# Squares' buffers moved to the front of SBUF in a fused block-attention and squared-ReLU kernel

## The chip, the cores and the metric

One NeuronCore of a Trainium2 chip. The metric is device time in microseconds (us) of one launch. The kernel before took 622.73 us (median of three runs, 622.30 to 624.28).

## The reference

Attention over q, k, v of shape (4 batches, 8 heads, 768 positions, 64), then a two-layer network on the 3072 tokens of width 512. Every query sees the keys less than 16 positions away and, besides, one summary of each 32-key block (the maximum of the keys, the mean of the values).

```python
k_sum = k.reshape(B, H, nb, block, D).max(axis=3)
v_sum = v.reshape(B, H, nb, block, D).mean(axis=3)
scores_all = np.concatenate([scores_l_m, scores_s], axis=-1)   # masked local, summary + log(32)
a = softmax(scores_all)
x = a @ np.concatenate([v, v_sum], axis=2)                     # (3072, 512) after the heads are joined
h = np.maximum(x @ w_in, 0.0)                                  # w_in (512, 2048)
out = (h * h) @ w_out                                          # w_out (2048, 512)
```

## The kernel before, in words

The 3072 tokens are 24 tiles of 128; two tiles make a chunk of 256 tokens, so there are 12 chunks. Every float32 matrix of the network is kept as a high and a low part in float32r, and a product is three matmuls: high by high, low weights by high, high weights by low.

**First layer** (`ffn1`, L384 to L393): for one of the 16 blocks f of 128 hidden units, 12 matmuls of 256 columns. The weights loaded into TensorE are 128 columns of `w_sb[f]`, the moving operand is a 256-column piece of `xh` or `xl` (L390). A slot does two f, so 24 matmuls. **Second layer** (`ffn2`, L427 to L437): for one f, two halves of 128 tokens by three matmuls of 512 columns. Here the weights loaded are 128 columns of the squares `gh` or `gl`, and the moving operand is the second half of a row of `w_sb[f]` (L434). A slot has 12 of them. Between the layers ScalarE takes the ReLU (L398) and the high square (L404), VectorE the square (L409) and its low part (L412).

For the first two chunks the order of every instruction is written out by hand in the string START (L42 to L69): weights are unpacked there and the attention of the first six tiles is done. After that `slot` (L468 on) runs 8 slots per chunk: 24 first-layer matmuls, then the 12 second-layer matmuls of the slot before, and beside them the attention of the two tiles that come next, which VectorE, ScalarE and GpSimd do; its matmuls (L277, L360) stand at the end of the 8 slots. `tc.manual_schedule` keeps this order on each engine.

**Where things lie in SBUF.** A pool lays its tiles one behind the other, in steps of 32 bytes per partition, in the order in which they are first asked for. Three pools follow each other: `const` (L86 to L110), `big` (18 slots of 8192 bytes, in which the unpacked weights `w_sb[f]` end up), and `work` (the small `nmx` and `total`, then `xh`, `xl`, `ob`). Tiles named gap are read and written by nothing and only take room. In the built program before, bytes from the start of a partition: `gh` 48128, `gl` 52224, the slots of `big` from 56896 on, `nmx` from 204352, `total` from 204544, `xh` 204768 and 208864, `xl` 212960 and 217056, `ob` from 221152 to 229344. Inside a weight slot the low part begins 4096 bytes, the second layer's half 2048 bytes, the next 128 columns 512 bytes further on; pieces of `xh` and `xl` and the four squares in `gh` and `gl` are 1024 bytes apart, the two token halves of a square 512.

`mask_max` (L297 to L308) takes a tile `nmx` from a ring of six for every half of a token tile's heads; `exponentials` (L310) reads it, `inverse` (L317 on) gives it back.

Of the kernel before, what the change touches and what calls it, by code (L numbers as in the profile page):

```python
# [11 lines left out]
F32 = mybir.dt.float32  # L12
F32R = mybir.dt.float32r
# [11 lines left out]
P = 128  # L25
# [3 lines left out]
CT = TPC * P  # L29
# [43 lines left out]
def attn_ffn_kernel(ctx: ExitStack, tc: tile.TileContext, q, k, kt, v, vt, x0, w, consts, out):  # L73
# [3 lines left out]
    const = ctx.enter_context(tc.tile_pool(name="const", bufs=1))  # L77
    big = ctx.enter_context(tc.tile_pool(name="big", bufs=1))
    work = ctx.enter_context(tc.tile_pool(name="work", bufs=2))
# [3 lines left out]


    w_sb = {}
    consts_sb = const.tile([P, 3 * NK + P + 8 * 32], F32, name="consts_sb")  # L86
    mask_sb = consts_sb[:, 0 : 3 * NK].rearrange("q (m c) -> q m c", m=3)
    id_sb, mean_sb = consts_sb[:, 3 * NK : 3 * NK + P], consts_sb[:, 3 * NK + P :]
# [9 lines left out]
    ksums = [const.tile([P, NPAIR, NB], F32, name=f"ksum{i}") for i in range(2)]  # L98
    vsum = const.tile([P, NPAIR, 32], F32, name="vsum")
    r_sb = [const.tile([P, DM], F32, name=f"r{i}") for i in range(2)]  # L100
    const.tile([P, 56], F32, name="gap0")
    gh_sb = const.tile([P, 4, CT], F32R, name="gh")
    gl_sb = const.tile([P, 4, CT], F32R, name="gl")

    sm_sb = const.tile([P, 8, 4, 2], F32, name="sm")
    zero = const.tile([P, 1], F32R, name="zero")
    zero32 = const.tile([P, 1], F32, name="zero32")
    junk = const.tile([P, 1], F32, name="junk")

    const.tile([P, 56], F32, name="gap")  # L110


    bank = [ps_s.tile([P, DM], F32, name=n, tag=f"{n}{i}") for i, n in enumerate(["s_ps"] * 4 + ["ph"] * 2)]
# [8 lines left out]
    def e_sb(g):  # L122
        return e_bufs[g % 2 if g < FROM_PAIRS else 0]
# [142 lines left out]
    s_ps, nmx, sm = {}, {}, {}  # L266
# [30 lines left out]
    def mask_max(g, h):  # L297

        t = g % NT
        m = mask_sb[:, 0 if t == 0 else 2 if t == NT - 1 else 1, :]  # L300
        half, i = divmod(h, 4)
        if (g, half) not in nmx:
            nmx[g, half] = work.tile([P, 4], F32, name="nmx", tag="nmx", bufs=6)
            sm[g, half] = sm_sb[:, (2 * g + half) % 8]
        nc.vector.tensor_tensor_reduce(  # L305
            out=e_sb(g)[:, h, 0:NK], in0=s_ps[g, half][h % 2][:, h // 2, 0:NK], in1=m, scale=-scale, scalar=3.0e38,
            op0=ALU.add, op1=ALU.min, accum_out=nmx[g, half][:, i : i + 1],
        )  # L308
# [8 lines left out]
    def softmax(g, h0, h1):  # L317

        for h in range(h0, h1):
            mask_max(g, h)  # L320
            exponentials(g, h)
# [250 lines left out]
    def begin(op, i, j, eng, at):  # L572
# [19 lines left out]
        elif op == "S":  # L592
            (scores_kt if i < FROM_KT else scores)(i, 2 * j, 2 * j + 2, at)
        elif op == "TT":
            mask_max(i, j)
        elif op == "E":
            exponentials(i, j)
# [150 lines left out]
```

## Time and profile before

| what | value |
|---|---|
| median of three runs | 622.73 us |
| the profiled execution's own time | 622.01 us |
| its span, first to last instruction | 619.9 us |
| TensorE matmuls busy | 607.6 us, 98% of the span |
| VectorE / ScalarE / GpSimd busy | 389.8 / 267.4 / 106.2 us |
| granted TensorE clock, mean | 0.999 of full speed |

A matmul's record includes its way through the array, and records overlap: TensorE's pace is the distance from one matmul's start to the next one's. The chain of work that ended last gives it without overlap, as stretches between starts.

### The profile page before, as it was taken

The numbers are of one execution on the slowest core, as the hardware profiler recorded it, in microseconds if no ns is written. First come the engines' busy times: TensorE is split into PE (matmuls) and PEld (weight loads), VectorE is DVE, ScalarE is ACT, GpSimd is POOL, SyncE is SP. The second block draws the span as 40 slices with busy tenths as digits, with TensorE's granted clock in tenths as the row PEclk, the third lists the DMA queues.
The fourth block names the chain that finished last, engine by engine and source line by source line (L and its number), as shares of the span: only waits on it lengthen the run. The fifth ranks groups of instructions, "written<-read, shape, count | busy, mean of one in ns | idle before, by whom it ended". The sixth has DMA issues, their size and how long they took to land.

```text
span 619.9 us, 12969 instructions
## 1 busy us (share of the span) xinstructions
PE 607.6 (98%) x5253; PEld 546.5 (88%) x5253; DVE 389.8 (63%) x1063; ACT 267.4 (43%) x688; POOL 106.2 (17%) x98
## 2 busy tenths in 40 slices
PE   7799999999999999999999999999999999999997
PEld 6589899789899999999999989999989989998996
DVE  6898998777637837747545845864663763663121
ACT  4898983234243432433425325425424424422212
POOL 4655466202000101102101101002101010110000
PEclk9999999999999999999999999999999999999999
DMA  8998141560007006006005204202201400300000
GB/s 329 410 413 336 52 136 52 153 193 30 1 9 264 2 2 220 2 2 221 1 2 188 86 1 126 97 1 76 95 2 38 133 1 1 87 1 1 35 1 34
DMA packets 21643, 59.41 MB, mean 96 GB/s; under 512 B 2256, under 2 KB 2256, under 8 KB 20048
## 3 DMA queue, kind: packets, MB, share of 16 engines
q1 hardware_dynamic: 21584, 58.59, 26.9%
q8 instruction: 41, 0.67, 0.4%
q14 instruction: 18, 0.15, 0.1%
HBM read 52.29 MB, written 6.29 MB: 94 GB/s over the span
## 4 chain that ended last, share of the span: by engine, by line
PE 93%; DVE 2%; ACT 2%; DMA 2%; SPq 1%; issue 0%; POOL 0%; DVEq 0%; POOLq 0%
PE o_ps L434 42%; PE ph L390 39%; PE s_ps L390 5%; PE ph L360 3%; PE s_ps L277 3%; DMA consts_sb<-in_consts 1%; ACT e_sb L313 1%; DVE w_sb L262 1%; PE s_ps L360 1%; DMA kv<-in_kt 0%; PE o_ps L159 0%; DVE v_sb L126 0%; SPq L180 0%; DVE ksum L188 0%; PE s_ps L339 0%
## 5 line engine op out<-in xcount | busy, mean ns | idle before, releaser
L390 PE MATMUL ph<-xh,w_sb 128*128 128x256 f32 x1360 | 246.8, 282 | 0.5 <-DVE xl L377 0.5
L434 PE MATMUL o_ps<-w_sb,gh 128*128 128x512 f32 x768 | 239.0, 392 | 0.0
L390 PEld LDWEIGHTS ph<-xh,w_sb 128*128 128x128 f32 x1360 | 213.4, 188 | 8.6 <-issue 1.4
L390 PE MATMUL ph<-xl,w_sb 128*128 128x256 f32 x680 | 190.5, 280 | 0.0
L434 PEld LDWEIGHTS o_ps<-w_sb,gh 128*128 128x128 f32 x768 | 137.6, 188 | 25.2 <-issue 0.2
L409 DVE TENSOR_TENSOR ph<-ph,r 128x512 f32<-128x512 f32 x83 | 58.1, 699 | 151.7 <-ACT r L398 150.9
L434 PE MATMUL o_ps<-w_sb,gl 128*128 128x512 f32 x384 | 151.2, 394 | 0.0
L398 ACT ACTIVATE r<-ph 128x512 f32<-128x512 f32 x83 | 49.2, 594 | 199.7 <-PE ph L390 199.7
L390 PEld LDWEIGHTS ph<-xl,w_sb 128*128 128x128 f32 x680 | 128.7, 189 | 0.0
L346 DVE STREAM_TRANSPOSE pT<-e_sb 32x256 f32<-32x256 f32 x240 | 104.6, 436 | 4.1 <-POOL e_sb L333 0.7
L313 ACT ACTIVATE e_sb<-e_sb,nmx 128x120 f32<-128x120 f32 x192 | 73.8, 386 | 68.8 <-DVE nmx L305 68.8
L333 POOL TENSOR_TENSOR e_sb<-e_sb,total 128x480 f32<-128x480 f32 x46 | 46.3, 1014 | 325.8 <-DVE total L327 181.3
L434 PEld LDWEIGHTS o_ps<-w_sb,gl 128*128 128x128 f32 x384 | 72.2, 188 | 15.3
L404 ACT ACTIVATE gh<-r 128x512 fp32r<-128x512 f32 x94 | 59.4, 632 | 11.9 <-DVE r L400 6.8
L412 DVE TENSOR_TENSOR gl<-ph,gh 128x512 fp32r<-128x512 f32 x83 | 57.4, 692 | 8.7 <-DVE ph L409 0.5
L253 POOL TENSOR_TENSOR w_raw<-w_raw 128x1024 int32<-128x1024 int32 (+1 forms) x20 | 34.1, 1712 | 35.6 <-DVE w_raw L248 18.1
L305 DVE CUSTOM_DVE_ANT_0 e_sb<-s_ps,consts_sb 128x120 f32<-128x120 f32 x172 | 38.8, 277 | 0.6 <-DMA consts_sb<-in_consts 0.2
L313 ACT ACTIVATION_READ_ACCUMULATOR e_sb<-e_sb,nmx 128x1 f32 x192 | 36.2, 188 | 0.0
L390 PE MATMUL s_ps<-xh,w_sb 128*128 128x256 f32 x176 | 32.5, 283 | 0.4 <-DVE w_sb L262 0.4
L390 PEld LDWEIGHTS s_ps<-xh,w_sb 128*128 128x128 f32 x176 | 27.5, 188 | 1.6 <-DVE w_sb L262 0.8
L377 DVE TENSOR_TENSOR xl<-ph,xh 128x512 fp32r<-128x512 f32 x19 | 13.1, 691 | 23.3 <-ACT xh L374 23.3
L390 PE MATMUL s_ps<-xl,w_sb 128*128 128x256 f32 x88 | 24.7, 281 | 0.0
(89 smaller groups left out, 419.0 us busy)
## 6 DMA issues: line engine op xcount, KB each, us to landing
w_raw<-in_w SPq DMA_DIRECT2D x12, 1024.0 KB, 11.7
k_sb<-in_k SPq DMA_DIRECT2D x20, 384.0 KB, 6.3
v_sb<-in_v SPq DMA_DIRECT2D x20, 384.0 KB, 4.7
kv<-in_kt SPq DMA_DIRECT2D x16, 384.0 KB, 5.7
q_sb<-in_q SPq DMA_DIRECT2D x24, 256.0 KB, 6.2
out<-ob SPq DMA_DIRECT2D x24, 256.0 KB, 2.1
kv<-in_vt SPq DMA_DIRECT2D x12, 384.0 KB, 6.3
w_raw<-in_w SPq DMA_DIRECT2D x8, 512.0 KB, 8.8
```

The costliest lines, as they stand in the source:

```text
L253: nc.gpsimd.tensor_tensor(out=lo, in0=hi, in1=lo, op=ALU.add)
L305: nc.vector.tensor_tensor_reduce(out=e_sb(g)[:, h, 0:NK], in0=s_ps[g, half][h % 2][:, h // 2, 0:NK], in1=m, scale=-scale, scalar=3.0e38, o ...
L313: nc.scalar.activation(e, e, AF.Exp, bias=nmx[g, half][:, i : i + 1], scale=-1.0, accum_out=sm[g, half][:, i, 0:1])
L333: eng.tensor_mul(out=e, in0=e, in1=sm.pop((g, half)).unsqueeze(2).to_broadcast([P, 4, NK]))
L346: nc.vector.transpose(out=pT[g % 2][j * 32 : j * 32 + 32, :, i * 32 : i * 32 + 32], in_=e_sb(g)[i * 32 : i * 32 + 32, :, j * 32 : j * 32 + ...
L360: nc.tensor.matmul(xp[o : o + 64, h // 2, s * 64 : s * 64 + 64], lhsT=values(g)[:, s, h * 64 : h * 64 + 64], rhs=pT[g % 2][:, h, s * 64 : ...
L390: nc.tensor.matmul(ph, lhsT=w_sb[f][:, w, cc * P : (cc + 1) * P], rhs=x[c][:, cc, :], start=(n == 0), stop=(n == 3 * NC4 - 1))
L398: nc.scalar.activation(r, ph, AF.Relu)
L404: nc.scalar.activation(gh, r, AF.Square)
L409: nc.vector.tensor_mul(out=ph, in0=ph, in1=r)
L412: nc.vector.tensor_sub(out=gl, in0=ph, in1=gh.bitcast(F32))
L434: nc.tensor.matmul(o_ps[c][tt], lhsT=g_[:, ts_], rhs=w_sb[f][:, w, DM:], start=(first and n == 0), stop=(last and n == 2),)
```

## The change

The two tiles of the squares move from behind the ReLU results to the front of the `const` pool, with a gap of 128 bytes ahead of them in place of one of 224; the gap at the end of that pool shrinks from 224 to 64 bytes; the ring of `nmx` gets a seventh tile. No instruction is added, taken away or moved.

```diff
     w_sb = {}
+    const.tile([P, 32], F32, name="gap0")
+    gh_sb = const.tile([P, 4, CT], F32R, name="gh")
+    gl_sb = const.tile([P, 4, CT], F32R, name="gl")
     consts_sb = const.tile([P, 3 * NK + P + 8 * 32], F32, name="consts_sb")
...
     r_sb = [const.tile([P, DM], F32, name=f"r{i}") for i in range(2)]
-    const.tile([P, 56], F32, name="gap0")
-    gh_sb = const.tile([P, 4, CT], F32R, name="gh")
-    gl_sb = const.tile([P, 4, CT], F32R, name="gl")
-
     sm_sb = const.tile([P, 8, 4, 2], F32, name="sm")
...
-    const.tile([P, 56], F32, name="gap")
+    const.tile([P, 16], F32, name="gap")
...
-            nmx[g, half] = work.tile([P, 4], F32, name="nmx", tag="nmx", bufs=6)
+            nmx[g, half] = work.tile([P, 4], F32, name="nmx", tag="nmx", bufs=7)
```

## Rows read from the trace of the kernel before

**Rows 1.** The profiled page: the span, TensorE's and the other engines' busy time, and the chain of work that ended last.
```profile
span 619.9 us, 12969 instructions
PE 607.6 (98%) x5253; PEld 546.5 (88%) x5253; DVE 389.8 (63%) x1063; ACT 267.4 (43%) x688; POOL 106.2 (17%) x98
...
PE 93%; DVE 2%; ACT 2%; DMA 2%; SPq 1%; issue 0%; POOL 0%; DVEq 0%; POOLq 0%
```

**Rows 2.** What TensorE waited for over the whole span, the longest two: us in total, times, longest.
```profile
PE s_ps L293 <- DMA q_sb<-in_q: 1.9, 2, 1.2
PE o_ps L566 <- issue: 1.3, 1, 1.3
```

**Rows 3.** Groups of instructions over the span, one form each: the matmuls of the two layers (busy us, mean ns | idle before).
```profile
L390 PE MATMUL ph<-xh,w_sb 128*128 128x256 f32 x1360 | 246.8, 282 | 0.5 <-DVE xl L377 0.5
L434 PE MATMUL o_ps<-w_sb,gh 128*128 128x512 f32 x768 | 239.0, 392 | 0.0
L390 PE MATMUL ph<-xl,w_sb 128*128 128x256 f32 x680 | 190.5, 280 | 0.0
L434 PE MATMUL o_ps<-w_sb,gl 128*128 128x512 f32 x384 | 151.2, 394 | 0.0
L390 PE MATMUL s_ps<-xh,w_sb 128*128 128x256 f32 x176 | 32.5, 283 | 0.4 <-DVE w_sb L262 0.4
L390 PE MATMUL s_ps<-xl,w_sb 128*128 128x256 f32 x88 | 24.7, 281 | 0.0
```

**Rows 4.** The chain in order of time in the middle and near the end of the steady stretch: start us, us, what.
```profile
331.35 2.85 PE ph L390 x24
334.19 2.76 PE o_ps L434 x12
...
602.25 2.85 PE ph L390 x24
605.10 2.76 PE o_ps L434 x12
```

**Rows 5.** Two stretches of the steady state, the second without attention: us, then busy us (x count) of PE, PEld, DVE, ACT, POOL, then the granted clock, DMA share and GB/s.
```profile
173.50:562.80 389.30, 388.82 (x3266) 352.67 (x3265) 235.93 (x687) 151.21 (x430) 34.81 (x38) 1.00 0.20 66
562.80:611.00 48.20, 48.20 (x314) 44.10 (x315) 11.83 (x17) 11.42 (x20) 0.00 (x0) 1.00 0.03 12
```

**Rows 6.** The timeline of TensorE at the start: 16 matmuls whose two operands are one broadcast zero, at the full clock (start us, us from the first start to the last end), and the last of them alone.
```profile
4.80 3.66 PE L566 MATMUL o_ps<-zero 128*128 128x512 f32 x16
...
8.08 0.38 PE L566 MATMUL o_ps<-zero 128*128 128x512 f32 x1
```

**Rows 7.** The timeline of TensorE over an ordinary first-layer slot: its third matmul, and the start of the second layer.
```profile
179.34 0.28 PE L390 MATMUL ph<-xl,w_sb 128*128 128x256 f32 x1
...
181.94 0.63 PE L434 MATMUL o_ps<-w_sb,gh 128*128 128x512 f32 x2
182.41 0.39 PE L434 MATMUL o_ps<-w_sb,gl 128*128 128x512 f32 x1
```

**Rows 8.** The same over the slot just before it, whose first matmuls came after those of the attention.
```profile
173.22 0.28 PE L277 MATMUL s_ps<-k_sb,q_sb 64*64 64x120 f32 x4
...
173.77 0.28 PE L390 MATMUL ph<-xl,w_sb 128*128 128x256 f32 x1
...
176.35 0.62 PE L434 MATMUL o_ps<-w_sb,gh 128*128 128x512 f32 x2
176.81 0.39 PE L434 MATMUL o_ps<-w_sb,gl 128*128 128x512 f32 x1
```

**Rows 9.** The same over a first-layer block of START, after a wait of TensorE for the unpacked weights.
```profile
68.32 0.39 PE L390 MATMUL s_ps<-xh,w_sb 128*128 128x256 f32 x1 [0.17 <-DVE w_sb L262]
68.54 0.28 PE L390 MATMUL s_ps<-xl,w_sb 128*128 128x256 f32 x1
...
69.74 0.63 PE L434 MATMUL o_ps<-w_sb,gh 128*128 128x512 f32 x2
```

**Rows 10.** The timeline of TensorE over one slot's second layer: the two token halves of one f, then of the next.
```profile
345.24 0.63 PE L434 MATMUL o_ps<-w_sb,gh 128*128 128x512 f32 x2
...
345.95 0.62 PE L434 MATMUL o_ps<-w_sb,gh 128*128 128x512 f32 x2
...
346.63 0.62 PE L434 MATMUL o_ps<-w_sb,gh 128*128 128x512 f32 x2
...
347.32 0.62 PE L434 MATMUL o_ps<-w_sb,gh 128*128 128x512 f32 x2
...
348.01 0.40 PE L390 MATMUL ph<-xh,w_sb 128*128 128x256 f32 x2
```

**Rows 11.** The records of the first layer's matmuls of `xh`: count, shortest/median/longest ns, first and last start, forms.
```profile
L390 PE MATMUL ph<-xh,w_sb x1360: 277/281/393, 35.2 to 610.3; 128*128 128x256 f32 x195
```

**Rows 12.** The line of `mask_max`: its instructions, and what its engine sat idle for before them (us, times).
```profile
L305 DVE CUSTOM_DVE_ANT_0 e_sb<-s_ps,consts_sb x172: 253/278/284, 10.7 to 543.7; 128x120 f32<-128x120 f32 x172
...
  DMA consts_sb<-in_consts: 0.2, 1
```

**Rows 13.** Groups of the page: the ReLU and the square between the layers (busy us, mean ns | idle of the engine before it and what ended most of that).
```profile
L409 DVE TENSOR_TENSOR ph<-ph,r 128x512 f32<-128x512 f32 x83 | 58.1, 699 | 151.7 <-ACT r L398 150.9
L398 ACT ACTIVATE r<-ph 128x512 f32<-128x512 f32 x83 | 49.2, 594 | 199.7 <-PE ph L390 199.7
```

## The prediction, written before the changed kernel was run

> **What bounds the kernel now.** I read the page first: matmuls are busy for 98% of the span, and the chain that ended last runs through TensorE for 93% of it [rows 1]. Next the waits of TensorE: the longest two sum to 3.2 us out of 619.9 [rows 2], so no other engine, queue or buffer can give back more than a few us. What is left is TensorE's own pace, so the third view is the chain in order of time, which counts from start to start. A slot of the steady state is 24 first-layer matmuls in 2.85 us and 12 second-layer matmuls in 2.76 us [rows 4]: 118.8 ns for 256 columns, 230 ns for 512. At the granted full clock of 2.4 GHz [rows 5] the columns alone are 106.7 and 213.3 ns. So each matmul loses 12 and 17 ns beyond its columns.
>
> Is that loss a fixed cost? Three views say no. (a) The matmuls of zeros at the start, with both operands broadcast from one element, start every (8.08 - 4.80) / 15 = 0.219 us [rows 6]: 5.4 ns beyond the columns, not 17. (b) The pace of the first layer depends on how it was entered. From the third matmul of an ordinary slot to the third of the second layer it is 182.41 - 179.34 = 3.07 us [rows 7]; in the slot entered from the attention's matmuls the same 24 distances take 176.81 - 173.77 = 3.04 [rows 8]; and in a block of START entered after a wait, ten distances take 69.74 - 68.54 = 1.20 us, 120 ns each [rows 9]. Same shapes, same clock, same offsets between operands, three paces. (c) It is not the other engines: the pace is 2.85 and 2.76 in the last 48 us too [rows 4], where VectorE is busy 11.8 and GpSimd 0 us [rows 5]. My reading: while one matmul streams its moving operand, the weights of the next are loaded, and the two reads disturb each other by their addresses and by their offset in time. The rows show the second of these; the first is inferred, and it is what the change acts on.
>
> **The change part by part.** It moves no instruction; the sum consists of what addresses do.
>
> *The new places.* From the tile sizes in steps of 32 bytes: the front now holds 128 + 8192 bytes more, so everything from `consts_sb` to `r` moves up by 8320. The weight slots begin at 56896 - 8192 - 224 - 224 + 8192 + 128 + 64 = 56640. `work` follows 256 bytes lower, less 32 for the seventh `nmx`: `xh` moves from 204768 to 204544. `gh` moves from 48128 to 1280. Distances:
> - `xh` minus weights: 147872 before, 147904 after. That is 32 bytes more, by any period: 416 becomes 448 modulo 512. All 2304 first-layer matmuls see it (1360 + 680 + 176 + 88 in [rows 3]).
> - weights minus `gh`: 8768 before, 55360 after. Modulo 512 both are 64; modulo 1024, 576 becomes 64. All 1152 second-layer matmuls (768 + 384 in [rows 3]).
> - `xl` minus `gh`, which meet once a slot where the second layer's first weights are loaded: 480 becomes 0 modulo 512.
>
> *Second layer: nothing.* The two token halves of a square lie 512 bytes apart, so before the change already half the matmuls stand at 576 and half at 64 modulo 1024. After the slot's first half, the halves take 346.63 - 345.95 = 0.68, 0.69 and 0.69 us [rows 10]: no difference between them. The move swaps which half has which distance. Bounds, were it otherwise: records in that group average 392 for `gh` and 394 ns for `gl` [rows 3]; 2 ns on 1152 is 2.3 us either way.
>
> *First layer: 32 bytes.* No row shows this distance, so I bound it. Below: the shortest record is 277 ns against a median of 281 [rows 11]; if every matmul lost only that, 4 x 2304 = 9.2 us gained. The pace of the zeros, 106.7 + 5.4 = 112.1 ns, would give (118.8 - 112.1) x 2304 = 15.4 us, but its operands stay on one element, so I keep it as a far end. Above: the pace of 120 ns [rows 9] everywhere costs 1.2 x 2304 = 2.8 us; no row of a whole block is slower. The value I take is the faster regime that this kernel already has when the two reads start at another offset [rows 8], since a shift of 32 bytes is a shift of offset between the reads too: 0.03 us for 24 distances. Of 2304 / 24 = 96 slots' worth, 12 (the first of each chunk) have it already, so 84 x 0.03 = 2.5 us. The readings are to 0.01 us, so it is 1.7 to 3.4.
>
> *The joint.* The first half of the second layer takes 345.95 - 345.24 = 0.71 us where later ones take 0.69 [rows 10]; with the new `xl` to `gh` distance the 0.02 us may go: 84 x 0.02 = 1.7 us at most, part of it counted in the 0.03 above. I take 0.7; the other bound is as much lost.
>
> *The seventh `nmx` and the gaps: nothing.* `mask_max` never sat idle for a buffer, only 0.2 us for a DMA [rows 12]. Tiles that nothing reads cost nothing.
>
> *Other engines' operands: nothing.* The squares are written by ScalarE and VectorE at other addresses. If that slowed them, the cover is large: ScalarE's ReLU stood idle 199.7 us waiting for TensorE, and VectorE's square 150.9 us for the ReLU [rows 13]. No DMA is added or reordered.
>
> The sum: 2.5 + 0.7 = 3.2 us less. The profiled execution took 622.01 us, 0.72 less than the median; 622.73 - 3.2 = 619.5 us.
>
> **The rivals.**
> *No change.* The two reads do not meet by address at all, and the three paces come from timing alone: whatever TensorE's reads wait for would then be the same at every distance, and the time 622.7 us. For it: slots at all 16 weights and both buffers of `xh` have the same 2.85 us [rows 4], and the second layer's halves agree across 512 bytes [rows 10]; it takes 32-byte effects to survive where 512-byte and larger ones do nothing. Against it: the zeros' pace [rows 6]. The Trainium skill ("SBUF — State Buffer", "Who interferes with whom") states a rule to the same end: TensorE has two independent read ports, one for the moving operand and one for loading weights, and never waits on anyone. By that rule the sum is 0 us. The trace neither confirms nor excludes it: three paces at one set of distances say that the two streams are coupled, not that addresses couple them.
>
> *Slower.* The new distance puts the ordinary slots into the slow regime. Place: L390's matmuls in all slots not entered from the attention. Price: 120 against 118.8 ns [rows 9, 4], 84 x 24 x 1.2 = 2.4 us, and the joint 0.7 lost instead of gained: 625.8 us. It decides as soon as the ordinary slot's 24 matmuls take over 2.86 us. For it: the slow regime lasts over a block once entered [rows 9], and a distance picked for other contents of SBUF has no reason to suit this one. Against: only one block of START is seen in it, while the fast one comes back at the head of every chunk [rows 8].
>
> *The change moves the second layer instead.* If the period of the effect is over 512 bytes after all, 230 ns changes by 2 to 4 ns: 2.3 to 4.6 us either way; shared out to the cases by sign.
>
> **How the numbers follow.** A measurement of this kernel tells 0.3% from no change, 1.9 us. Faster by more: 0.47, because the fast regime is in the trace and the room below (9.2, at the far end 15.4 us) is wider than above (2.8 to 4.6). Within 1.9 us: 0.25, the first rival and small shifts. Slower by more: 0.28. The predicted time is that of the likeliest case, 619.5 us, whose own range is 612 to 620.8. The whole range reaches up over no change to the slow regime with the second layer's bound on top, 622.7 + 2.4 + 0.7 + 2.3 = 628.1, and down to 622.7 - 9.2 - 1.7 = 611.8: 612 to 628 us.
>
> **What would show it.** In the chain of the changed kernel the ordinary slot's first-layer stretch of 24 should read 2.82 us, and the second layer's 12 stay at 2.75 to 2.76. If 24 read 2.85 and 2.76 again, the first rival holds; 2.88 is the second. If 12 matmuls of the second layer move from 2.76 by more than 0.02, my reading of the 512-byte period was wrong. If TensorE's pace is unchanged and the time is not, it must show as a wait of TensorE that is not in [rows 2], and all of the above is wrong.

## The result

613.17 us (median of four runs, 612.82 to 613.26) against 622.61 (now four runs of the kernel before): ratio 0.984, 95% interval 0.982 to 0.986. The profiled execution took 612.82 us with a span of 610.7, 9.2 us less than before [rows 1]. So the change made the kernel faster by about 1.5%, inside the range of the forecast and on its side, but by 9.4 us where 3.2 were forecast. The granted clock is 0.999 in the profiles of both kernels.

### The profile page after: what moved, and what is told of

The parts are those of the page before. It is cut to its first block, busy times and chain, and to the rows that moved or that the text cites. A ratio compares the mean times of both kernels' runs of the same rounds, so it can differ in the third digit from the quotient of the medians.

```text
span 610.7 us, 12969 instructions
## 1 busy us (share of the span) xinstructions
PE 598.4 (98%) x5253; PEld 537.8 (88%) x5253; DVE 389.8 (64%) x1063; ACT 267.5 (44%) x688; POOL 106.3 (17%) x98
## 4 chain that ended last, share of the span: by engine, by line
PE 91%; DVE 3%; ACT 3%; DMA 2%; issue 1%; SPq 0%; POOL 0%; DVEq 0%; ACTq 0%; POOLq 0%
PE o_ps L433 42%; PE ph L389 38%; PE s_ps L389 3%; PE ph L359 3%; PE s_ps L276 3%; DVE w_sb L261 1%; ACT e_sb L312 1%; DMA q_sb<-in_q 1%; PE s_ps L359 1%; ACT w_raw L236 1%; DMA kv<-in_kt 1%; PE o_ps L158 0%; DVE v_sb L125 0%; SPq L179 0%; DVE ksum L187 0%
## 5 line engine op out<-in xcount | busy, mean ns | idle before, releaser
L389 PE MATMUL ph<-xh,w_sb 128*128 128x256 f32 x1360 | 239.3, 278 | 0.6 <-DVE xl L376 0.5
L433 PE MATMUL o_ps<-w_sb,gh 128*128 128x512 f32 x768 | 238.0, 391 | 0.0
L389 PEld LDWEIGHTS ph<-xh,w_sb 128*128 128x128 f32 x1360 | 211.0, 188 | 8.9 <-issue 1.4
L389 PE MATMUL ph<-xl,w_sb 128*128 128x256 f32 x680 | 188.3, 277 | 0.0
L433 PEld LDWEIGHTS o_ps<-w_sb,gh 128*128 128x128 f32 x768 | 137.1, 188 | 25.1 <-issue 0.2
L433 PE MATMUL o_ps<-w_sb,gl 128*128 128x512 f32 x384 | 151.3, 394 | 0.0
L389 PEld LDWEIGHTS ph<-xl,w_sb 128*128 128x128 f32 x680 | 127.8, 188 | 0.0
L433 PEld LDWEIGHTS o_ps<-w_sb,gl 128*128 128x128 f32 x384 | 72.2, 188 | 14.6 <-DVE gl L411 0.3
L389 PE MATMUL s_ps<-xh,w_sb 128*128 128x256 f32 x176 | 31.5, 279 | 0.7 <-DVE w_sb L261 0.7
L389 PEld LDWEIGHTS s_ps<-xh,w_sb 128*128 128x128 f32 x176 | 27.1, 188 | 1.9 <-DVE w_sb L261 1.1
L389 PE MATMUL s_ps<-xl,w_sb 128*128 128x256 f32 x88 | 24.4, 277 | 0.0
```

Of the source, the lines that this page charges most:

```text
L389: nc.tensor.matmul(ph, lhsT=w_sb[f][:, w, cc * P : (cc + 1) * P], rhs=x[c][:, cc, :], start=(n == 0), stop=(n == 3 * NC4 - 1))
L433: nc.tensor.matmul(o_ps[c][tt], lhsT=g_[:, ts_], rhs=w_sb[f][:, w, DM:], start=(first and n == 0), stop=(last and n == 2),)
```

## The profile after the change

The page of the changed kernel: span, busy time, then the first layer's groups (L389 and L433 are the lines that were L390 and L434), to be set beside [rows 1, 3].

```profile
span 610.7 us, 12969 instructions
PE 598.4 (98%) x5253; PEld 537.8 (88%) x5253; DVE 389.8 (64%) x1063; ACT 267.5 (44%) x688; POOL 106.3 (17%) x98
...
L389 PE MATMUL ph<-xh,w_sb 128*128 128x256 f32 x1360 | 239.3, 278 | 0.6 <-DVE xl L376 0.5
L433 PE MATMUL o_ps<-w_sb,gh 128*128 128x512 f32 x768 | 238.0, 391 | 0.0
L389 PE MATMUL ph<-xl,w_sb 128*128 128x256 f32 x680 | 188.3, 277 | 0.0
L433 PE MATMUL o_ps<-w_sb,gl 128*128 128x512 f32 x384 | 151.3, 394 | 0.0
```

The counts are the same and the other engines work as long as before; the first layer's mean record went from 282 and 280 to 278 and 277 ns. The chain in order of time, as in [rows 4]:

```profile
129.62 2.94 PE ph L389 x24
132.56 2.75 PE o_ps L433 x12
...
338.13 2.75 PE ph L389 x24
340.88 2.75 PE o_ps L433 x12
343.62 2.75 PE ph L389 x24
...
593.29 2.75 PE ph L389 x24
596.04 2.75 PE o_ps L433 x12
```

A slot is 5.49 to 5.50 us where it was 5.61: 0.10 from the first layer, 0.01 from the second. In the kernel before, the first steady slot began here:

```profile
130.28 3.02 PE ph L390 x24
```

From there to the end it took 619.9 - 130.28 = 489.6 us, now 610.7 - 129.62 = 481.1: 8.5 of the 9.2 us lie in the 80 steady slots (80 x 0.11 = 8.8), 0.7 in START. Inside one slot, the timeline of TensorE, as in [rows 7]:

```profile
177.84 0.28 PE L389 MATMUL ph<-xl,w_sb 128*128 128x256 f32 x1
...
178.54 0.28 PE L389 MATMUL ph<-xl,w_sb 128*128 128x256 f32 x1
...
180.24 0.28 PE L389 MATMUL ph<-xl,w_sb 128*128 128x256 f32 x1
180.35 0.62 PE L433 MATMUL o_ps<-w_sb,gh 128*128 128x512 f32 x2
180.81 0.39 PE L433 MATMUL o_ps<-w_sb,gl 128*128 128x512 f32 x1
181.04 0.62 PE L433 MATMUL o_ps<-w_sb,gh 128*128 128x512 f32 x2
```

From 178.54 to 180.24 are 15 distances: 113.3 ns each, 1.2 above the 112.1 worked out from the zeros [rows 6]. The six distances before it take 0.70 us, 117 ns each: a slot begins at about the old pace and within its first matmuls locks into the new one. The second layer's first half takes 181.04 - 180.35 = 0.69 us where it took 0.71 [rows 10].

## The experiments

Distances are modulo 512 bytes: X is `xh` minus weights, Y is weights minus `gh`. The kernel before has X 416, Y 64; the changed one X 448, Y 64. The theory: X and Y set the paces, because the moving operand and the next weights are read at once. Its rivals are named where they are tested.

**Which part of the change does it?** Three kernels. The seventh ring tile without moving the squares (from the kernel before):

```diff
-    const.tile([P, 56], F32, name="gap0")
+    const.tile([P, 40], F32, name="gap0")
...
-            nmx[g, half] = work.tile([P, 4], F32, name="nmx", tag="nmx", bufs=6)
+            nmx[g, half] = work.tile([P, 4], F32, name="nmx", tag="nmx", bufs=7)
```

> The squares stay behind the ReLU results, as before; the nmx ring gets its seventh tile and the gap ahead of the squares is 64 bytes smaller, so that xh minus weights is 147904 (448 modulo 512, as in the changed kernel) and weights minus gh 8768 (as before). Distance theory (moving operand to weights decides): the whole gain is here, 24 first-layer matmuls in 2.75 us, 12 second-layer ones in 2.75, about 613 us. Alignment theory (xh begins at a multiple of 64 bytes): the same, since xh is at 204736. Squares theory (their place at the front, 64 instead of 576 modulo 1024, decides): 2.85 and 2.76, 622 us.

The same with 48 in place of 40 floats, so that the same distances begin 32 bytes off a multiple of 64:

> As the kernel before, with a seventh nmx tile and the gap ahead of the squares 32 bytes smaller: weights and squares lie 32 bytes lower, xh and xl stay at 204768 and 212960. Distances as in the run with the seventh tile and 64 bytes less (448 and 64 modulo 512), but every one of these tiles now begins 32 bytes off a multiple of 64. Distance theory: 2.75 us for 24, about 613 us. Alignment theory: 2.85 us, 622 us.

And the changed kernel with the ring back at six:

```diff
-            nmx[g, half] = work.tile([P, 4], F32, name="nmx", tag="nmx", bufs=7)
+            nmx[g, half] = work.tile([P, 4], F32, name="nmx", tag="nmx", bufs=6)
```

> The changed kernel with six nmx tiles again, so that xh and xl lie 32 bytes lower: xh minus weights 416 modulo 512 as before, squares at the front. Distance theory: the gain is gone, 2.85 us for 24 and about 622 us. Alignment theory: gone as well, xh is at 204512. Squares theory: the gain stays, 2.75 us and 613 us.

Measured: 613.04 (ratio 0.984, 0.981 to 0.986), 613.10 (0.984, 0.982 to 0.986) and 622.24 us (0.999, 0.998 to 1.001). The chains, in this order:

```profile
333.14 2.75 PE ph L390 x24
335.89 2.75 PE o_ps L434 x12
```

```profile
332.96 2.75 PE ph L390 x24
335.71 2.75 PE o_ps L434 x12
```

```profile
331.08 2.85 PE ph L389 x24
333.93 2.76 PE o_ps L433 x12
```

The 32 bytes between `xh` and the weights are the whole change. Moving the squares to the front gave nothing by itself, and neither did a multiple of 64. Nor is it the seventh buffer as such: the kernels below with seven tiles and X 256, 320 or 64 take 620.6 to 623.8 us. The joint's 0.01 us comes and goes with the same 32 bytes; since `xl` minus `gh` moves with X in these three kernels, what it hangs on is not separated here.

**Is it the two reads?** The kernel before at its own distances, with the first layer's weights loaded from one broadcast zero, then with its moving operand a broadcast zero:

```diff
-ph, lhsT=w_sb[f][:, w, cc * P : (cc + 1) * P], rhs=x[c][:, cc, :], start=(n == 0),
+ph, lhsT=zero.to_broadcast([P, P]), rhs=x[c][:, cc, :], start=(n == 0),
...
+ph, lhsT=w_sb[f][:, w, cc * P : (cc + 1) * P], rhs=zero.to_broadcast([P, CT]), start=(n == 0),
```

> The kernel before, all places as they were (416 and 64), but the first layer loads its weights from one broadcast zero, so that the output is not the network's: the load touches one element and the moving operand is read as ever. Two-reads theory: no collision is left in the first layer, 24 in 2.69 us (112.1 ns, the pace of the zeros) to 2.72 us although the distance is the bad one. Rival (the moving operand's own read, or accumulating in PSUM, costs the 12 ns): 2.85 us. The second layer 2.75 to 2.76 by both.

> The same the other way round: the first layer loads its real weights and streams one broadcast zero as moving operand (xh and xl are computed and not used, the output is not the network's). Two-reads theory: 2.69 to 2.72 us for 24. Rival (loading the weights sets the pace by itself): 2.85 us. If this one falls and the run with zero weights does not, it is the moving operand's own read.

Measured, one run each: 615.41 and 609.02 us. The chains:

```profile
333.81 2.80 PE ph L390 x24
336.61 2.75 PE o_ps L434 x12
339.36 2.73 PE ph L390 x24
```

```profile
333.65 2.76 PE o_ps L434 x12
336.41 2.68 PE ph L390 x24
339.10 2.77 PE o_ps L434 x12
```

With the moving operand on one element the loss is gone: 2.68 us, the pace of the zeros (24 x 112.1 = 2.69), although the weights are loaded as before. With the weights on one element 0.05 to 0.12 of the 0.17 us go. The expectation for zero weights (2.69 to 2.72) missed. So the loss needs the moving operand's own read; the load's part is not measured by this pair, since a load that stays on one element still reads it. That the weights' place counts is shown by the second of the three kernels above: there `xh` stayed at 204768, the weights moved by 32 bytes, and the 24 matmuls went from 2.85 to 2.75 us. In both runs here an operand is zero in value too. The squares that the second layer loads are then zero as well, and its 12 matmuls still take 2.75 to 2.77 us, so zero values speed nothing up there; for the first layer this was not tested by itself.

**The first layer's distance.** The changed kernel with eight and with nine ring tiles (X 480 and 0):

> The changed kernel with eight nmx tiles: xh minus weights 480 instead of 448 modulo 512, nothing else but xl minus gh, 32 instead of 0. Distance theory, with 448 one good place on a curve: another 32 bytes change the first layer's stretch of 24 again, to anything from 2.70 (every distance 112 ns) to 2.88 us; 607 to 624 us. Rival (32 bytes off 416 were harmful and all other distances are alike): 2.75 us, 613 us.

> The changed kernel with nine nmx tiles: xh minus weights 0 modulo 512, so that the moving operand and the weights loaded meanwhile start together. Distance theory: if closeness to the other stream is what hurts, this is the worst, 2.85 us or more for 24 and 622 us or more; if 448 is the edge of a wide good stretch, 2.75 us and 613 us.

Measured 621.25 us (0.996, 0.994 to 0.999) and 625.40 (1.005, 1.002 to 1.008):

```profile
334.41 2.75 PE o_ps L433 x12
337.16 2.84 PE ph L389 x24
```

```profile
330.25 2.75 PE o_ps L433 x12
333.00 2.88 PE ph L389 x24
```

448 is no edge of a wide good stretch: 32 bytes on, nearly everything is lost, and 64 bytes on it is worse than before.

**The second layer's distance.** The changed kernel with the gap ahead of the weights at 0, 8, 24 and 32 floats instead of 16 (Y 0, 32, 96, 128), and with `sm` placed ahead of the squares and a gap of 48 floats (Y 448):

```diff
-    const.tile([P, 16], F32, name="gap")
+    const.tile([P, 8], F32, name="gap")
```

> The changed kernel without the gap ahead of the weights: weights minus gh 0 instead of 64 modulo 512, xh minus weights still 448. Distance theory: only the second layer's pace moves (at 448 it went from 229 to 233 ns), to anything between 219 and 236 ns, 12 in 2.62 to 2.83 us, and with it the joint. Rival (its pace is what it is except at 448): 2.75 and 2.75, 613 us.

> The changed kernel with weights minus gh 32 instead of 64 modulo 512 (xh minus weights 448). The second layer took 226.7 ns at 0, 228.9 at 64: 227 to 229 here by the distance theory, 12 in 2.72 to 2.75. Whether the first layer stays at 113.3 ns (as at 64), alternates (as at 128 and 448) or stays at 117.8 (as at 0) shows whether its regime hangs on the second layer's end: if the fast regime stays, about 612 us; if not, 616 to 618 us.

> The changed kernel with weights minus gh 96 instead of 64 modulo 512. Distance theory for the second layer: between 228.9 ns at 64 and 231.7 at 128, 12 in 2.75 to 2.78. First layer: fast throughout gives 613 to 616 us, alternating 616 to 618 us.

> The changed kernel with the gap ahead of the weights 64 bytes larger: weights minus gh 128 instead of 64 modulo 512. As for the run with distance 0, on the other side: the second layer's 12 in 2.62 to 2.83 us by the distance theory, and of the two one should be better than 2.75 if 64 is not the best place; 2.75 by the rival.

> The changed kernel with the small tile sm ahead of the squares and the gap behind them 128 bytes larger: weights minus gh is 448 instead of 64 modulo 512, xl minus gh 384 instead of 0, xh minus weights stays 448. Distance theory, which must hold for the second layer too: its matmuls now have the moving operand 448 above the loaded weights, the first layer's good distance, so 12 of them fall from 2.75 towards 12 x 0.219 = 2.62 us, 0.13 x 96 = 12 us, about 601 us, and the first layer keeps 2.75. Rival (the second layer's 229 ns are its own cost, whatever the addresses): 2.75 and 2.75, 613 us. Squares theory: the first layer falls back to 2.85, 622 us.

Measured in this order: 616.31, 623.56, 617.81, 618.31 and 620.18 us. The chains of 0, 96 and 128:

```profile
334.39 2.83 PE ph L388 x24
337.22 2.72 PE o_ps L432 x12
339.94 2.83 PE ph L388 x24
```

```profile
334.79 2.75 PE ph L389 x24
337.54 2.80 PE o_ps L433 x12
340.33 2.75 PE ph L389 x24
```

```profile
335.13 2.83 PE ph L389 x24
337.95 2.78 PE o_ps L433 x12
340.73 2.73 PE ph L389 x24
343.46 2.77 PE o_ps L433 x12
```

The second layer obeys its own distance, 2.72 to 2.80 us, but not smoothly: at 32 and at 96 it takes 2.80, where 2.72 to 2.75 and 2.75 to 2.78 were expected from the neighbours. The hope that the first layer's good distance suits it as well (448: 2.80) was wrong. And a thing no theory had: at the same X 448 the first layer has two paces, 2.73 to 2.75 and 2.83 us, and how a block is entered decides which. At Y 64 and 96 it is fast in every slot, at 128 and 448 in every other one, at 0 and 32 only where a chunk begins, after the attention's matmuls. For Y 0, a first slot of a chunk, which takes 2.94 us in the changed kernel too, and the next slot:

```profile
220.98 2.94 PE ph L388 x24
...
226.66 2.83 PE ph L388 x24
```

The alternation is not that of the two buffers which slots use in turn: at Y 448 the second slot of a chunk takes 2.83 us in one chunk and 2.73 in the next. So the second layer's best place (2.72) was paid for by the first layer.

**Period, and a better version.** With `xh` and `xl` asked for first, a pad ahead of them, and `sm` and the gaps as the distance needs:

```diff
+    work.tile([P, 64], F32, name="pad", tag="pad", bufs=1)
+    work.tile([P, NPAIR, CT], F32R, name="xh", tag="xh")
+    work.tile([P, NPAIR, CT], F32R, name="xl", tag="xl")
```

> The changed kernel with xh and xl asked for first in their pool, behind a pad of 256 bytes, and no gap ahead of the weights: xh minus weights 256, weights minus gh 0 modulo 512. The second layer should repeat its 226.7 ns at 0 (12 in 2.72). First layer, if nearness of the two streams at their start is what hurts (120.0 ns at 0): half a period off is the best place, 112 to 113 ns throughout, 24 in 2.70 to 2.74 and 608 to 611 us. If 448 is a single good place: 117 to 120 ns, 2.82 to 2.88 us, 615 to 622 us.

> In the same way xh minus weights 128 and weights minus gh 192 modulo 512. Smooth curve: the second layer, 231.7 ns at 128, goes on up to 233 or turns down towards 227; the first layer lies between its 120.0 at 0 and whatever 256 gives. If only differences of 64 bytes from the start count, as the second layer's 233.7 at 32 and 228.9 at 64 suggest, no such order.

> xh minus weights 320, weights minus gh 256 modulo 512, xl minus gh 64. If the period is 256 bytes and not 512, the second layer repeats the 226.7 ns of distance 0 and the first layer behaves as at 64; if it is 512, both are new values.

> xh minus weights 64, weights minus gh 320 modulo 512. With a period of 256 bytes the second layer repeats the 228.9 ns of 64, and the first layer the value of the run at 320. The first layer at 64 is the mirror of 448 (64 above instead of 64 below): 113 to 118 ns if the sign does not matter, about 120 if it does.

Measured: 623.76, 625.87, 620.69 and 620.61 us. The chain of the first; for the third (X 320, Y 256) a line of its chain and the end of a second layer in its timeline; and the same end in the run with Y 0:

```profile
337.74 2.87 PE ph L391 x24
340.61 2.75 PE o_ps L435 x12
```

```profile
330.57 2.83 PE ph L390 x24
...
194.60 0.39 PE L434 MATMUL o_ps<-w_sb,gl 128*128 128x512 f32 x1
...
195.28 0.39 PE L434 MATMUL o_ps<-w_sb,gl 128*128 128x512 f32 x1
```

```profile
193.91 0.39 PE L432 MATMUL o_ps<-w_sb,gl 128*128 128x512 f32 x1
...
194.59 0.39 PE L432 MATMUL o_ps<-w_sb,gl 128*128 128x512 f32 x1
```

X 256 runs as X 0 did (2.87 and 2.88), X 320 as X 64 (2.83 both), and three matmuls at the end of the second layer take 0.68 us at Y 256 as at Y 0: the period is 256 bytes. The starts in the traces, which are kept to a nanosecond, say the same more sharply: averaged over the ordinary slots, the second layer ends in steps of 227 ns at Y 0 and 256, and in a repeating 226, 229, 232 ns in the kernel before, the changed one (both Y 64) and at Y 320. Half of that, 128 bytes, is no period: X 0 and 128 differ (2.88 and 2.84 to 2.85), X 64 and 192 too. At Y 0 and 256 the 227 ns come only after a few matmuls when X is not 448, so the whole 12 take 2.75 and 2.76 us in the first and third run here, and the 2.72 expected of the first was missed. X 256, half of a period of 512, was not the best place but one of the worst.

Last, two attempts to have the second layer's 2.72 and the first layer's 2.75 together:

```diff
-    const.tile([P, 16], F32, name="gap")
...
+    const.tile([P, 16], F32, name="gap1")
     gl_sb = const.tile([P, 4, CT], F32R, name="gl")
```

> The changed kernel with the 64 bytes of the gap ahead of the weights moved between gh and gl: weights minus gh stays 64, weights minus gl becomes 0, xh minus weights 448. If the second layer's pace is a mean over its loads by distance, one load in three moves from the 64 kind to the 0 kind: 228.9 - 2.2 / 3 = 228.2 ns. If the first layer's fast regime needs the end that the second layer has at 64: kept, 24 in 2.75 us, about 612.3 us; if one load at 0 already spoils it: 2.83 us and 619 us.

```diff
-    const.tile([P, 16], F32, name="gap")
...
-            x[c] = work.tile([P, NPAIR, CT], F32R, name=name, tag=name)
+            if not x_all:
+                x_all.append(work.tile([P, 4 * DM * TPC + 8], F32R, name="x_all", bufs=1))
+            o4 = 4 + (c % 2 + 2 * (name == "xl")) * DM * TPC
+            x[c] = x_all[0][:, o4 : o4 + DM * TPC].rearrange("p (a b) -> p a b", a=NPAIR)
```

> The changed kernel without the gap ahead of the weights (weights minus gh and gl 0, second layer 226.7 ns as measured) and with xh and xl in one tile that begins 16 bytes further on: xh minus weights 464 modulo 512, between the good 448 and the bad 480. If 448 is the edge of a good stretch that 464 is inside of, the first layer is fast from any entry, 24 in 2.72 to 2.75 us: 613.2 - 1152 x 2.2 ns = 610.6 us. If the good place is 448 alone: 117 to 118 ns, 2.83 us, 616 to 617 us.

Measured 616.63 us (0.990, 0.987 to 0.992) and 622.08 (1.000, 0.998 to 1.002):

```profile
334.65 2.74 PE ph L389 x24
337.39 2.79 PE o_ps L433 x12
```

```profile
336.63 2.86 PE ph L393 x24
339.49 2.73 PE o_ps L437 x12
```

Both missed in time. A `gl` at another distance than `gh` makes the second layer slower than either place alone (2.79); the first layer stays fast, as hoped, except where a chunk begins (3.02 for 2.94 us). And 16 bytes past 448 the first layer takes 2.86. No version tried beats the changed kernel; the one with the seventh tile and the squares still behind the ReLU results equals it (613.04). All places together (us for 24 and 12; the changed kernel's line is the second):

| X mod 256 | Y mod 256 | first layer | second layer | median us |
|---|---|---|---|---|
| 160 (before) | 64 | 2.85 | 2.76 | 622.6 |
| 192 (after) | 64 | 2.75 | 2.75 | 613.2 |
| 208 | 0 | 2.86 | 2.73 | 622.1 |
| 224 | 64 | 2.84 | 2.75 | 621.3 |
| 0 | 64 | 2.88 | 2.75 | 625.4 |
| 0 | 0 | 2.87 | 2.75 | 623.8 |
| 64 | 0 | 2.83 | 2.76 | 620.7 |
| 64 | 64 | 2.82 to 2.83 | 2.75 to 2.77 | 620.6 |
| 128 | 192 | 2.84 to 2.85 | 2.79 to 2.80 | 625.9 |
| 192 | 0 | 2.83 | 2.72 | 616.3 |
| 192 | 32 | 2.83 | 2.80 | 623.6 |
| 192 | 96 | 2.75 | 2.80 | 617.8 |
| 192 | 128 | 2.83 and 2.73 | 2.77 to 2.78 | 618.3 |
| 192 | 192 | 2.83 and 2.74 | 2.79 to 2.80 | 620.2 |

One more rival falls by this table: that the distance between `xl` and `gh`, which is X + Y, sets the first layer's pace. It is 0 in the changed kernel, but 32 at Y 96, where the first layer is as fast, and 0 again at X 0, Y 0, where it takes 2.87.

## Why the prediction was right and wrong

*What bounds the kernel*: right. TensorE's waits stayed small, the longest two 2.7 us after 3.2 before, and the time moved by its pace.

*Addresses couple the two reads*: inferred then, shown now. 32 bytes of distance move the pace back and forth, absolute places do not, and with the moving operand on one element the loss is gone at the bad distance. This decides the first rival. What was counted for that one, that steps of 512 bytes and more do nothing, is what a period of 256 gives. The Trainium skill ("SBUF — State Buffer", "Who interferes with whom") has TensorE's two read ports as independent and TensorE as never waiting on anyone: the measurement disagrees, 2.75 against 2.85 us for the same 24 matmuls.

*Second layer: nothing*: right for this change, 2.75 for 2.76 us. The reason given was right too: 512 bytes do nothing, since the period is 256, and the kernel with the seventh tile and the squares still behind, at 576 modulo 1024 as before, takes the same 2.75. With that the third rival falls.

*First layer: 32 bytes*: the step that failed, in its size. I took 0.03 us per 24, the faster regime of the trace before [rows 8]; measured are 0.10, 2.75 us where 2.82 was to be seen. The bound that I had kept as a far end, because the operands of the zeros stay on one element, was the near one: of the 6.7 ns between 118.8 and 112.1, a good place gives back 5.5 once it is locked in. The regime of [rows 8] was a phase at a bad distance and says little of a good one. The first slots of a chunk were said to have the gain already; they gained 0.08 (3.02 to 2.94). The steady stretch has 10 of them, not 12, and 70 ordinary slots, which give 7.0 us; the first slots, START and the joint make up the 9.2. That the sign was right is in good part luck: of the seven distances modulo 256 that were run, 192 alone is under 2.82, and nothing in [rows 8] pointed to it. That the span shrank by just the 9.2 us of the nearer bound, 4 ns for every matmul, is in part chance too: locked in, a matmul gains 5.5, the first ones of a slot gain less, and the joint is in the 9.2.

*The joint*: 0.7 us taken, 0.01 to 0.02 us a slot measured, about 1 us; that `xl` minus `gh` is the reason was not shown.

*`nmx`, gaps, other engines*: right. VectorE and ScalarE are busy as long as before, 389.8 and 267.5 us.

*The second rival*, a slower regime from the new place, did not happen here, but it was no empty one: X 0 (2.88) and Y 0 (2.83 at the same X) show slower regimes from a new place. Two of the pairs in the table, at 625.4 and 625.9 us, are slower than before by 0.5%.

What stays open: why 192 and no neighbour, and what makes the two reads disturb each other with a period of 256 bytes; nothing here shows it. That the way a block is entered picks the first layer's regime is seen, not explained.

## What to carry to other kernels

When TensorE never waits and its matmuls still start later than their columns need, compare with matmuls on one broadcast element in the same trace: that shows how much there may be to gain. No place tried here beat it: the first layer came within 1.2 ns of it, the second no nearer than 8 (226.7 against 218.7). Then try the distance between the moving operand and the weights loaded meanwhile in small steps (32 bytes here), one layer at a time but judged by the whole slot, since a block's pace hangs on what ran before it. A tile added or dropped between the two operands changes their distance, while one ahead of both moves both, as the squares at the front did. So a change of buffers that should be free is worth a look at start-to-start times.

## What the runs showed of the hardware that was not expected

The pace of 256-column matmuls lies between 113 and 120 ns by the place of their operands and by how the block was entered (2.73 to 2.88 us for 24), that of 512-column ones between 227 and 233 ns (2.72 to 2.80 for 12), with a period of 256 bytes. At one and the same distance a block can lock into the faster pace or stay at the slower one to its last matmul, 2.73 or 2.83 us, by how it was entered.
